# Turning the first x chunks on TensorE instead of in the DMA, in a fused linear-attention and FFN kernel

## The chip, the core and the metric

The kernel runs on one core of a Trainium2 chip. The metric is the device time of one execution in microseconds. The core has TensorE (PE: matmuls; PEld is its weight load, which overlaps the matmuls), VectorE (DVE), ScalarE (ACT), GpSimd (POOL) and SyncE (SP), which here only issues DMAs. Every engine has its own instruction stream, and the streams are tied together by semaphores. A DMA is issued by one engine's queue (SP's or ScalarE's here), moved by 16 DMA engines that all queues share, and tells of its landing by a semaphore.

## What is computed

The input x has 2048 tokens of 640 features in bf16. The output mixes two branches with a gate for each token: linear attention with a learned softmax feature map over 32 heads of 20 features, and a SwiGLU feed-forward net of width 1728.

```python
qkv = x @ wqkv                       # 32 heads, 20 features each
pq, pk = q @ w_phi, k @ w_phi        # per head
phi = concat(softmax(p), softmax(-p))
kv, z = phi_k^T @ v, sum(phi_k)
a = (phi_q @ kv / (phi_q @ z + 1e-6)) @ wo
b = (silu(x @ w_gate) * (x @ w_up)) @ w_down
g = sigmoid(sum(x * gate_w))
return g * a + (1 - g) * b
```

## The kernel before

**Layout.** All matmuls contract over the partitions, so x is needed with its features on the partitions: xT holds five chunks of 128 features by 2048 tokens. x lies in memory with the tokens first. Six DMA transposes bring it (line 515), by blocks of 512 tokens; the first block comes in three pieces, chunks 0 and 1, chunks 2 and 3, chunk 4. The weights w_gate and w_up (wg, wu) are loaded in pieces by chunk and by column, `k` being a block of 128 columns.

**Order.** The order of every engine's instructions is fixed when the program is built. `_Plan` (lines 238 to 334) is a list scheduler: each task has an engine, an estimated cost, dependencies, a priority, and sometimes an `after` (the task that must precede it on its engine), a `hold` (not before this planned time) or a `land` (when a DMA is taken to have landed). The planner walks through its own time, and emits each task's instructions when its turn comes. What the chip then does is bound to the order, not to the planned times: `_Tracker` (line 38) puts a semaphore wait ahead of an instruction wherever it reads or overwrites what another engine or DMA produced. The constants `L_SLACK`, `E_SLACK` and `O_SLACK` (line 484) are added to planned landings of loads and of two kinds of transposes; lines 713 to 720 hold planned start times of the key tiles (`K_AT`, `K_EACH`), of the query tiles (`Q_AT`, `Q_EACH`), ranks (`PRE_Q`), and how the feed-forward's down projections are threaded among the rest (`D_AFTER`).

**The head.** The loads of lines 540 to 564 are all issued by SP, one after another. The first are wg[0:2] for four blocks k (line 540), x chunks 0 and 1 transposed (541), wu[0:2] (542), wg[2:5] for k 0 and 1 (543), x chunks 2 to 4 transposed (544), wg[2:5] for k 2 and 3 (545), wu[2:5] (546), then the next weight pieces and the second block of x (547, 548). Meanwhile PE runs ten warm matmuls on a row of ones (lines 610 to 622), which compute nothing that is used. `ffn_head` (line 684) then computes gate and up projections of the first 512 tokens for four blocks k, in all eight PSUM banks, chunk by chunk in the order in which the pieces arrive: 8 matmuls for wg[0:2], 8 for wu[0:2], 4 and 2 for wg[2:4] and wg[4:5] with k 0 and 1, 6 for wg[2:5] with k 2 and 3, 12 for wu[2:5]. ScalarE (tanh), VectorE and GpSimd finish each block (`ffn_tail`, line 636).

**The rest.** Interleaved by the planner follow the rest of the feed-forward, value and key tiles, then the query tiles. In each query tile the features are normalised, transposed by a DMA (`eT`), multiplied with the key-value matrix, divided, transposed again (`oT`) and multiplied with wo. Scratch tensors that are needed only early (wqT, wbd, wph) share the slab in which the output tiles (xsb) are later collected (lines 403 to 409).

Of the kernel before, what the change touches and what calls it, by code (L numbers as in the profile page):

```python
# [6 lines left out]
P = 128  # L7
S_TOK = 2048
D = 640
H = 32  # L10
DH = 20
F_FFN = 1728
NT = S_TOK // P
# [12 lines left out]
PC = 6 * DH  # L26
NPC_W = 6
PHI_NH = (6, 6, 6, 6, 6, 2)
ACTF = mybir.ActivationFunctionType
ALU = mybir.AluOpType  # L30
AX = mybir.AxisListType
DT = mybir.dt
BF16 = DT.bfloat16
# [204 lines left out]
class _Plan:  # L238
# [11 lines left out]
    def add(self, eng, cost, fn, deps=(), prio=5.0, lat=None, acq=(), rel=(), name=""):  # L250
        t = _Task(eng, cost, fn, deps, prio, self.LAT[eng] if lat is None else lat,
                  tuple(acq), tuple(rel), len(self.tasks), name)
        self.tasks.append(t)
        return t
# [86 lines left out]
def _build(  # L341
# [13 lines left out]
    pe, act, dve, pool, sp = nc.tensor, nc.scalar, nc.vector, nc.gpsimd, nc.sync  # L355
# [13 lines left out]
    def sbat(name, shape, dtype, at):  # L369
        t = nc.alloc_sbuf_tensor_at(name, list(shape), dtype, offset=at)  # L370
        tr.reg_tensor(t, "sbuf", at, rowelems(shape), mybir.dt.size(dtype))
        return t

    xT = sb("xT", [P, 5, S_TOK], BF16)
# [29 lines left out]
    base = nc.lookup_mloc(slab).addr  # L404
# [2 lines left out]
    wqT = sbat("wqT", [P, 2 * NPC_W, D], BF16, base)  # L407
    wbd = sbat("wbd", [P, NPC_W, 6, DH], BF16, base + 2 * NPC_W * D * 2)
    wph = sbat("wph", [PC, NPC_W, DH], BF16, base + 2 * NPC_W * D * 2 + NPC_W * 6 * DH * 2)

    ps = nc.alloc_psum_tensor("ps", [P, 8 * 512], F32)
    tr.addr[ps.name] = ("psum", 0, 8 * 512, 4)

    x2 = A_x[0]
# [3 lines left out]
    add = plan.add  # L418
# [4 lines left out]
    def one(b, c0, c1, r0=0, r1=P):  # L423
        return ps[r0:r1, b * 512 + c0:b * 512 + c1]
# [4 lines left out]
    def mms(groups):  # L429

        reads = [g[1] for g in groups] + [g[2] for g in groups]
        writes = []
        seen = set()
        for g in groups:
            k = (g[0].offset, str(g[0].ap))
            if k not in seen:
                seen.add(k)
                writes.append(g[0])

        def fn():  # L440
            last = None
            for o, l, r, st, sp_ in groups:
                last = pe.matmul(o, lhsT=l, rhs=r, start=st, stop=sp_, skip_group_check=True)  # L443
            return last
        run("pe", fn, reads=reads, writes=writes)
# [5 lines left out]
    def actop(o, i, func, scale=1.0):  # L451
        reads = [i] + ([scale] if isinstance(scale, bass.AP) else [])
        run("act", lambda: act.activation(o, i, func, scale=scale), reads=reads, writes=[o])  # L453

    def dveop(fn, reads, writes):
        run("dve", fn, reads=reads, writes=writes)

    def poolop(fn, reads, writes):
        run("pool", fn, reads=reads, writes=writes)

    def memset(t_ap, val, eng):
        eobj = {"pool": pool, "dve": dve}[eng]
        run(eng, lambda: eobj.memset(t_ap, val), reads=[], writes=[t_ap])
# [17 lines left out]
    v1ones = places(v1all)[:, :, :, DH]  # L481
    v1pad = v1all.rearrange("p (g x) -> p g x", x=WIN)[:, :, WIN - 1]

    L_SLACK, E_SLACK, O_SLACK = 1.0, 1.8, 1.6
    chain = {}

    def load(eng, dst, src, land, prio, transpose=False, name="load", cost=0.06):

        t = add(eng, cost, lambda: dma(eng, dst, src, transpose=transpose), prio=prio, lat=2.0, name=name)
        t.land = land  # L490
        t.slack = L_SLACK if land > 13 else 0.0
        t.after = chain.get(eng)
        chain[eng] = t
        return t

    def rows(a):
        return a.rearrange("(c p) j -> p c j", p=P)
# [4 lines left out]
    wgl = [None] * (NPC + 1)  # L502
    wul = [None] * (NPC + 1)

    def load_gu(j, eng, land, prio):
        c0, c1 = PIECES[j]
        wgl[j] = load(eng, wg[:, :, c0:c1], gsrc[:, :, c0:c1], land[0], prio)
        wul[j] = load(eng, wu[:, :, c0:c1], usrc[:, :, c0:c1], land[1], prio + 0.1)

    def load_x(bt, prio, *cuts):  # L510

        tok = slice(512 * bt, 512 * bt + 512)
        out_ = []
        for i, (c0, c1, land) in enumerate(cuts):
            out_ += [load("sp", xT[:, c0:c1, tok], x2[tok, c0 * P:c1 * P], land, prio + 0.1 * i, True, "x%d" % bt)] * (c1 - c0)
        return out_

    def load_wT(which, land, prio):
        o = NPC_W * which
        col = [which * D + PC * c for c in range(NPC_W)]  # L520
        return [load("sp", wqT[:, o + c, :], A_wqkv[:, col[c]:col[c] + P], land - 1.0 * (NPC_W - 1 - c), prio + 0.01 * c, True, "wT") for c in range(NPC_W)]
# [8 lines left out]
    xs = [None] * NBT  # L530
    HD = 4
    hw = {}

    def load_head(key, c0, c1, k0, k1, land, prio):
        w, src = (wg, gsrc) if key == "g" else (wu, usrc)
        t = load("sp", w[:, c0:c1, k0 * P:k1 * P], src[:, c0:c1, k0 * P:k1 * P], land, prio)
        for k in range(k0, k1):
            hw[key, c0, k] = t
        return t
    load_head("g", 0, 2, 0, HD, 3.9, -43)  # L540
    xa = load_x(0, -42, (0, 2, 5.25))
    load_head("u", 0, 2, 0, HD, 6.9, -41)
    load_head("g", 2, 5, 0, 2, 7.4, -40.5)
    xs[0] = xa + load_x(0, -40, (2, 4, 8.8), (4, 5, 9.3))
    wgl[0] = load_head("g", 2, 5, 2, HD, 10.0, -39.5)
    wul[0] = load_head("u", 2, 5, 0, HD, 11.3, -39)
    load_gu(1, "sp", (12.5, 13.7), -37)
    xs[1] = load_x(1, -36.5, (0, 5, 16.4))
    phi_rows = A_w_phi.rearrange("h e f -> (h e) f")
    ph_l = [load("sp", wph[:, 0:5, :], phi_rows[0:5 * PC, :].rearrange("(c p) j -> p c j", p=PC), 16.5, -36.2),  # L550
            load("sp", wph[0:2 * DH, 5, :], phi_rows[5 * PC:D, :], 16.6, -36.1)]
    wkT_l = load_wT(1, 24.4, -36)
    wv_l = load("sp", wvg[:, :, 0:D], rows(A_wqkv[:, 2 * D:3 * D]), 26.8, -35)
    load_gu(2, "sp", (28.0, 29.2), -34)
    load_gu(3, "sp", (30.6, 32.0), -33)
# [9 lines left out]
    xl = [x_[4] for x_ in xs]  # L565

    zero = add("dve", 0.3, lambda: memset(us[:, 0, 0:2], 0.0, "dve"), prio=-20, name="zero")
    table = add("act", 1.3, lambda: actop(us[:, 1, 0:1], us[:, 0, 0:1], ACTF.Tanh), deps=[zero], prio=-20, name="table")  # L570
# [39 lines left out]
    def warm(banks, before):  # L610
        ctx = {}

        def fn():
            for b in banks:
                last = pe.matmul(one(b, 0, 512), lhsT=ones_row[:, 0:P], rhs=ones_row[:, 0:512], start=True, stop=True, skip_group_check=True)
            return last
        b0, b1 = min(banks), max(banks) + 1
        t = add("pe", 0.427 * len(banks), lambda: run("pe", fn, reads=[], writes=[ps[:, b0 * 512:b1 * 512]]), prio=-10,
                acq=[("bank", ctx, i) for i in range(b0, b1)], rel=[("bank", ctx, i) for i in range(b0, b1)], name="warm")
        t.after = before  # L620
        return t
    warm_t = warm((4, 5, 6, 7, 4, 5), warm((0, 1, 2, 3), None))


    gate_t = {}
# [58 lines left out]
    def ffn_head():  # L684
        tsl = slice(0, 512)
        cs = [{} for _ in range(HD)]
        before = warm_t
        last = {}

        def group(key, c0, c1, parts):  # L690
            nonlocal before
            w = wg if key == "g" else wu

            def fn(ks, cc):
                mms([(one(cs[k][key], 0, 512), w[:, c, P * k:P * k + P], xT[:, c, tsl], c == 0, c == 4) for c in cc for k in ks])
            for ks in parts:
                t = add("pe", _mm(*[512] * (len(ks) * (c1 - c0))), lambda ks=ks: fn(ks, range(c0, c1)),
                        deps=[xs[0][c1 - 1], hw[key, min(c0, 2), ks[-1]]], prio=-5,
                        acq=[("bank", cs[k], key) for k in ks] if c0 == 0 else (), name="head")
                t.after = before  # L700
                before = t
                for k in ks:
                    last[key, k] = t
        group("g", 0, 2, [(0, 1, 2, 3)])
        group("u", 0, 2, [(0, 1, 2, 3)])
        group("g", 2, 4, [(0, 1)])
        group("g", 4, 5, [(0, 1)])
        group("g", 2, 5, [(2, 3)])
        group("u", 2, 5, [(0,), (1,), (2,), (3,)])
        for k in range(HD):  # L710
            ffn_tail(0, k, cs[k], (last["g", k], last["u", k]), 0)

    B_FIRST = 8
    K_AT, K_EACH, Q_AT, Q_EACH = 29.00, 6.115, 119.64, 8.094
    PRE_Q = 10.05
    PRE_EACH = 2.0
    PRE_AT = 23.6
    D_AFTER = 3
    FIN_DVE = 12
    K_PAIRS = 9  # L720
    store_t = {}
# [297 lines left out]
    pre_k = premult(1, wkT_l, 2.0, at=PRE_AT)  # L1019
    pre_q = premult(0, wqT_l, PRE_Q, 0.02)  # L1020
    wq_done[0] = pre_q[-1]
# [9 lines left out]
    for bt in range(1, NBT):  # L1031
        ks = list(range(K_PAIRS if bt == 1 else 0, NK))
        ds = [("d", u, bt - 1) for u in range(4)]
        for i, k in enumerate(ks):
            seq.append(("f", k, bt))
            if i >= D_AFTER and ds:
                seq.append(ds.pop(0))
# [67 lines left out]
```

## Time and profile before

| What | Value |
|---|---|
| Time, median of 3 runs | 287.14 us (287.12 to 287.69) |
| Profiled execution, its own time | 287.02 us |
| Profiled execution, span from first to last instruction | 285.3 us |
| TensorE's granted clock | 1.000 |
| PE 128x512 matmul of the head, x528 | 379 ns each by the record, one started every 216 |
| Line 909, POOL, normalising the features, x32 | 77.6 us in all |
| Line 899, DVE, summing the features, x32 | 48.5 us in all |
| DMA, 24.23 MB | mean 85 GB/s over the span |

The profile is of one execution. An engine's busy share says how much of the span it worked. A timeline line gives start, length, engine, line of the program, operation, out<-in and how many instructions are merged. A matmul's record lasts longer than the time until the next can start, since matmuls are pipelined, so starts are to be compared, not lengths. In the tables by stretch, each line is a stretch in us, its length, then busy time and number of instructions of PE, PEld, DVE, ACT and POOL, the granted clock, the DMA engines' mean share and the GB/s. SPq and ACTq are the issuing queues of SyncE and ScalarE. PE's 40 head matmuls run from 4.88 to 13.80 us, and its last five matmuls from 282.51 to 282.95; a last VectorE operation and a store follow.

### The profile page before, as it was taken

The page shows a single profiled execution, that of the slowest core. Times are in us where ns is not written, and L with a number is a line of the kernel's source. Part 1 is how long each engine was busy: PE and PEld are TensorE (multiplying, and loading weights), DVE is VectorE, ACT ScalarE, POOL GpSimd, SP SyncE. Part 2 cuts the span into 40 slices and gives each one's busy share as a digit, 9 for nine tenths or more (in the row PEclk, how much of TensorE's full clock was granted, in tenths as well). Part 3 has the DMA queues.
Part 4 walks back from the last instruction along what each step waited for, and adds up shares of the span by engine and source line. Part 5 has one row for each costly group of instructions (what it writes and reads, how often), then busy time and mean ns, then how long its engine had stood idle before and what let it go on. Part 6 is the DMA issues. An engine that isn't in the chain of part 4 may idle for free.

```text
span 285.3 us, 5120 instructions
## 1 busy us (share of the span) xinstructions
PE 279.9 (98%) x2013; PEld 150.6 (53%) x2050; DVE 224.0 (79%) x318; ACT 145.5 (51%) x222; POOL 171.1 (60%) x168
## 2 busy tenths in 40 slices
PE   8999999999999999999999999999999999999996
PEld 3444555555545455655465555555545555445654
DVE  1324398998999997997999999899989898961312
ACT  2555567685566484334634454745655444662210
POOL 5199406839657666745675577697786656575100
DMA  7979997860000000000302447473444254033211
GB/s 171 262 124 241 202 211 150 255 201 0 2 0 2 0 2 0 2 0 0 53 2 52 97 102 117 75 141 77 99 97 77 60 112 88 11 76 74 71 46 46
DMA packets 67457, 24.23 MB, mean 85 GB/s; under 512 B 55593, under 2 KB 67433, under 8 KB 67433
## 3 DMA queue, kind: packets, MB, share of 16 engines
q1 hardware_dynamic: 66777, 23.91, 40.0%
q8 instruction: 16, 0.26, 0.4%
q10 hardware_dynamic: 656, 0.00, 0.1%
q14 instruction: 8, 0.07, 0.1%
HBM read 8.30 MB, written 2.62 MB: 38 GB/s over the span
## 4 chain that ended last, share of the span: by engine, by line
PE 95%; SPq 2%; DMA 1%; issue 1%; DVE 0%
PE ps L443 95%; SPq L471 2%; DMA wg<-in_B_w_gate_dram 1%; DVE xsb L745 0%
## 5 line engine op out<-in xcount | busy, mean ns | idle before, releaser
L909 POOL TENSOR_TENSOR phi<-phi,rc 128x1320 bf16<-128x1320 bf16 x32 | 77.6, 2425 | 32.7 <-DVE rc L903 32.7
L661 POOL TENSOR_TENSOR hT<-hT,us 128x512 bf16<-128x512 bf16 (+1 forms) x56 | 64.0, 1152 | 45.4 <-DVE hT L655 31.1
L443 PE MATMUL ps<-xT,wg 128*128 128x512 bf16 x271 | 67.3, 379 | 0.8
L443 PE MATMUL ps<-xT,wu 128*128 128x512 bf16 x257 | 63.6, 379 | 0.0
L443 PE MATMUL ps<-wd,hT 128*128 128x512 bf16 (+1 forms) x442 | 62.2, 298 | 0.3
L453 ACT ACTIVATE phi<-phi 128x1320 bf16<-128x1320 bf16 x32 | 41.7, 1303 | 24.9 <-DVE phi L888 24.9
L453 ACT ACTIVATE hT<-ps 128x512 bf16<-128x512 f32 (+1 forms) x56 | 33.2, 597 | 41.1 <-PE ps L443 40.8
L899 DVE TENSOR_REDUCE sm<-phi 128x66 f32<-128x1320 bf16 x32 | 48.5, 1518 | 5.7 <-ACT phi L453 5.4
L655 DVE SCALAR_TENSOR_TENSOR hT<-hT,ps 128x512 bf16<-128x512 bf16 (+1 forms) x56 | 37.5, 675 | 18.8 <-ACT hT L453 18.8
L443 PEld LDWEIGHTS ps<-wd,hT 128*128 128x128 bf16 x448 | 35.1, 98 | 27.6
L443 PE MATMUL ps<-wqk,xT 128*128 128x128 bf16 (+1 forms) x311 | 47.4, 297 | 0.5
L453 ACT ACTIVATE us<-ps 128x512 bf16<-128x512 f32 (+1 forms) x56 | 33.2, 598 | 17.6 <-PE ps L443 16.3
L443 PEld LDWEIGHTS ps<-xT,wu 128*128 128x128 bf16 x260 | 25.3, 98 | 30.8 <-DMA wu<-in_B_w_up_dram 0.3
L443 PEld LDWEIGHTS ps<-xT,wg 128*128 128x128 bf16 x280 | 25.5, 98 | 26.2 <-DMA wg<-in_B_w_gate_dram 0.6
L443 PEld LDWEIGHTS ps<-wqk,xT 128*128 128x128 bf16 x320 | 26.1, 98 | 21.0
L876 DVE TENSOR_REDUCE mx<-ps 128x33 f32<-128x660 f32 x32 | 26.6, 832 | 6.8 <-PE ps L443 6.8
L888 DVE TENSOR_TENSOR phi<-mn,ps 128x660 bf16<-128x660 f32 x32 | 26.3, 822 | 0.3
L884 DVE TENSOR_TENSOR phi<-ps,mx 128x660 bf16<-128x660 f32 x32 | 26.4, 825 | 0.0
L880 DVE TENSOR_REDUCE mn<-ps 128x33 f32<-128x660 f32 x32 | 26.2, 817 | 0.0
L453 ACT ACTIVATE xsb<-ps,gs 128x640 bf16<-128x640 f32 x16 | 12.7, 793 | 25.3 <-PE ps L443 25.3
L759 POOL TENSOR_TENSOR xsb<-xsb,xb 128x640 bf16<-128x640 bf16 x12 | 16.7, 1396 | 11.3 <-ACT xb L453 11.3
L443 PE MATMUL ps<-wo,oT 128*128 128x128 bf16 (+1 forms) x153 | 23.0, 295 | 0.4
(45 smaller groups left out, 187.1 us busy)
## 6 DMA issues: line engine op xcount, KB each, us to landing
out_dram<-xsb SPq DMA_DIRECT2D x15, 160.0 KB, 1.9
wd<-in_B_w_down_dram SPq DMA_DIRECT2D x1, 2080.0 KB, 10.5
wvg<-in_A_wqkv_dram SPq DMA_DIRECT2D x1, 800.0 KB, 5.9
wg<-in_B_w_gate_dram SPq DMA_DIRECT2D x2, 400.0 KB, 6.4
wu<-in_B_w_up_dram SPq DMA_DIRECT2D x2, 400.0 KB, 6.7
wo<-in_A_wo_dram SPq DMA_DIRECT2D x1, 800.0 KB, 10.9
wg<-in_B_w_gate_dram SPq DMA_DIRECT2D x2, 320.0 KB, 5.5
wu<-in_B_w_up_dram SPq DMA_DIRECT2D x2, 320.0 KB, 6.1
```

Source lines behind the costliest of these rows:

```text
L443: last = pe.matmul(o, lhsT=l, rhs=r, start=st, stop=sp_, skip_group_check=True)
L453: run("act", lambda: act.activation(o, i, func, scale=scale), reads=reads, writes=[o])
L471: fn = (lambda: eobj.dma_start(dst, src, transpose=True)) if transpose else (lambda: eobj.dma_start(dst, src))
L655: dveop(lambda: dve.scalar_tensor_tensor(out=hap, in0=hap, scalar=1.0, in1=g_, op0=ALU.add, op1=ALU.mult), [hap, g_], [hap])
L661: poolop(lambda: pool.tensor_tensor(hap, hap, u_, ALU.mult), [hap, u_], [hap])
L759: poolop(lambda: pool.tensor_tensor(x_, x_, b_, ALU.add), [x_, b_], [x_])
L876: dveop(lambda: dve.tensor_reduce(a, b, AX.X, ALU.max), [b], [a])
L880: dveop(lambda: dve.tensor_reduce(a, b, AX.X, ALU.min), [b], [a])
L884: dveop(lambda: dve.tensor_tensor(o_, a, b, ALU.subtract), [a, mx[:, ctx["st"], :]], [o_])
L888: dveop(lambda: dve.tensor_tensor(o_, a, b, ALU.subtract), [b, mn[:, ctx["st"], :]], [o_])
L899: dveop(lambda: dve.tensor_reduce(a, b, AX.X, ALU.add), [b], [a])
L909: poolop(lambda: pool.tensor_tensor(a, a, b, ALU.mult), [a, r], [a])
```

## The change

The first two chunks of x's first 512 tokens are no longer transposed by a DMA. Two plain DMAs on SP bring them with tokens on the partitions (xp, 4 tiles of 128 by 128 for each chunk, in rows of 256 bytes). PE turns each tile by a matmul against an identity matrix into PSUM; VectorE copies the first half of the tokens into xT, ScalarE the second. GpSimd builds the identity. xp and the identity lie in the slab. w_gate's first piece is split in two, one for each chunk, and ScalarE's queue issues both. The first gate group is split likewise. Of the ten warm matmuls six are left. The planned landings of the head's loads and several planner constants have new values.

```diff
-    L_SLACK, E_SLACK, O_SLACK = 1.0, 1.8, 1.6
+    L_SLACK, E_SLACK, O_SLACK = 1.0, 1.6, 1.4
...
-    load_head("g", 0, 2, 0, HD, 3.9, -43)
-    xa = load_x(0, -42, (0, 2, 5.25))
-    load_head("u", 0, 2, 0, HD, 6.9, -41)
-    load_head("g", 2, 5, 0, 2, 7.4, -40.5)
-    xs[0] = xa + load_x(0, -40, (2, 4, 8.8), (4, 5, 9.3))
-    wgl[0] = load_head("g", 2, 5, 2, HD, 10.0, -39.5)
-    wul[0] = load_head("u", 2, 5, 0, HD, 11.3, -39)
...
+    def load_xp(c, land, prio):
+        return load("sp", xp[:, c, :, :], x2[0:512, c * P:(c + 1) * P].rearrange("(t p) j -> p t j", p=P), land, prio)
+    load_head("g", 0, 1, 0, HD, 3.4, -43, "act")
+    load_head("g", 1, 2, 0, HD, 4.2, -42.9, "act")
+    xp_l = [load_xp(0, 3.35, -43), load_xp(1, 3.8, -42)]
+    load_head("u", 0, 2, 0, HD, 5.2, -41)
+    load_head("g", 2, 5, 0, 2, 5.8, -40.5)
+    xs[0] = [None, None] + load_x(0, -40, (2, 4, 7.3), (4, 5, 7.9))
+    wgl[0] = load_head("g", 2, 5, 2, HD, 8.9, -39.5)
+    wul[0] = load_head("u", 2, 5, 0, HD, 10.1, -39)
...
+    def build_ident():
+        memset(ident[:, :], 1.0, "pool")
+        for m, b in ((1, 0), (-1, 0)):
+            poolop(lambda m=m: pool.affine_select(
+                out=ident[:, :], in_=ident[:, :], pattern=[[-m, P]], compare_op=ALU.is_ge, fill=0.0,
+                base=0, channel_multiplier=m), [ident[:, :]], [ident[:, :]])
+    ident_t = add("pool", 0.8, build_ident, prio=-30, name="ident")
...
-    warm_t = warm((4, 5, 6, 7, 4, 5), warm((0, 1, 2, 3), None))
+    warm_t = warm((4, 5, 6, 7), warm((0, 1), None))
+
+    def turn(c, before):
+        ctx = {}
+
+        def fn():
+            mms([(one(ctx[i // 2], P * (i % 2), P * (i % 2) + P), xp[:, c, i, :], ident[:, :], True, True) for i in range(4)])
+        t = add("pe", 0.43, fn, deps=[xp_l[c], ident_t], prio=-10, acq=[("bank", ctx, 0), ("bank", ctx, 1)], name="turn")
+        t.after = before
...
+        ev.append(add("dve", 0.36, copy_d, deps=[t], prio=-30, rel=[("bank", ctx, 0)], name="turned"))
+        ev.append(add("act", 0.36, copy_a, deps=[t], prio=-30, rel=[("bank", ctx, 1)], name="turned"))
+        return t, ev
+    turn_t, xe0 = turn(0, warm_t)
+    turn_t, xe1 = turn(1, turn_t)
+    xe = [xe0, xe1]
...
-        group("g", 0, 2, [(0, 1, 2, 3)])
+        group("g", 0, 1, [(0, 1, 2, 3)])
+        group("g", 1, 2, [(0, 1, 2, 3)])
...
-    K_AT, K_EACH, Q_AT, Q_EACH = 29.00, 6.115, 119.64, 8.094
-    PRE_Q = 10.05
+    K_AT, K_EACH, Q_AT, Q_EACH = 29.00, 6.110, 120.29, 8.074
+    PRE_Q = 10.12
...
-    D_AFTER = 3
+    D_AFTER = 4
```

## The prediction, made before the changed kernel ran

> **What bounds the kernel now.** I read the page first: its busy shares, then the chain that ended last.
>
> ```profile
> span 285.3 us, 5120 instructions
> PE 279.9 (98%) x2013; PEld 150.6 (53%) x2050; DVE 224.0 (79%) x318; ACT 145.5 (51%) x222; POOL 171.1 (60%) x168
> PE 95%; SPq 2%; DMA 1%; issue 1%; DVE 0%
> ```
>
> TensorE is busy 98% of the span and makes 95% of the chain. Only the first few microseconds belong to something else (SP's issues and one DMA). Next, the busy time by stretches of 20 us:
>
> ```profile
> 64.00:84.00 20.00, 19.84 (x155) 10.82 (x157) 19.05 (x25) 12.33 (x23) 14.38 (x12) 1.00 0.00 1
> 104.00:124.00 20.00, 19.85 (x164) 11.20 (x167) 18.11 (x25) 9.35 (x14) 11.59 (x11) 1.00 0.01 2
> 224.00:244.00 20.00, 19.84 (x161) 11.23 (x162) 17.15 (x26) 10.22 (x13) 10.76 (x9) 1.00 0.46 97
> ```
>
> The first figure after the length is PE. It is 19.8 of 20 everywhere, and the 0.16 left over is three pauses of 0.05, which the chain calls issue. So from the head's end on nothing waits, and nothing can be won there; something can be lost. What can be won lies ahead of 13.8 us. The timeline of PE:
>
> ```profile
> 3.36 0.99 PE L615 MATMUL ps<-const-bfloat16-1.0 128*128 128x512 bf16 x2
> ...
> 3.79 1.00 PE L615 MATMUL ps<-const-bfloat16-1.0 128*128 128x512 bf16 x3
> 4.88 1.89 PE L443 MATMUL ps<-xT,wg 128*128 128x512 bf16 x8
> 6.61 1.89 PE L443 MATMUL ps<-xT,wu 128*128 128x512 bf16 x8
> 8.33 3.04 PE L443 MATMUL ps<-xT,wg 128*128 128x512 bf16 x12
> 11.21 2.54 PE L443 MATMUL ps<-xT,wu 128*128 128x512 bf16 x11
> 13.80 1.24 PE L443 MATMUL ps<-xT,wg 128*128 128x512 bf16 x5
> ```
>
> L615 are the ten warm matmuls on ones, L443 is work. Eight matmuls take 6.61 - 4.88 = 1.73 us, 0.216 each. Warm ones follow each other at 0.427 (3.36 to 3.79) until about 4.2 us, so the array runs at half its rate that long. The head's 40 matmuls need 40 x 0.216 = 8.64 us, but 4.88 to 13.80 is 8.92: 0.28 us of waiting. The waits name it:
>
> ```profile
> PEld ps L443 <- DMA wg<-in_B_w_gate_dram: 0.6, 1, 0.6
> ...
> PEld ps L443 <- DMA wu<-in_B_w_up_dram: 0.3, 1, 0.3
> ```
>
> The first is the piece wg[2:5, k 2-3], whose wait ends at 9.90 (the weight loader's 0.6 is partly under a running matmul). Last, what the DMA engines moved, by microsecond (the last two figures are DMA share and GB/s):
>
> ```profile
> 2.00:3.00 1.00, 1.00 (x4) 0.36 (x3) 0.45 (x3) 0.30 (x2) 0.86 (x4) 1.00 0.79 199
> 3.00:4.00 1.00, 1.00 (x4) 0.38 (x3) 0.63 (x2) 0.00 (x0) 0.86 (x4) 1.00 1.20 290
> 4.00:5.00 1.00, 0.91 (x4) 0.23 (x3) 0.00 (x0) 0.00 (x0) 0.61 (x2) 1.00 0.80 138
> 5.00:6.00 1.00, 1.00 (x6) 0.43 (x5) 0.00 (x0) 0.00 (x0) 0.00 (x0) 1.00 0.98 281
> ```
>
> At full stream the loads make 280 to 290 GB/s, with transposes (3 to 4) and without (5 to 6). Behind the transposed x chunks the rate falls to 138 (126 in 4.0 to 4.9).
>
> **The sum as a rule.** The head's end is the later of two: start T plus 8.64 if no weight is late, or the old 13.80 less s, where s is by how much the stream brings wg[2:5, k 2-3] earlier (18 matmuls stand behind that piece either way). Gain = the smaller of 13.80 - 8.64 - T = 5.16 - T, and s.
>
> **T, the start of useful work.** The six warm matmuls left end at about 0.84 + 0.38 + 5 x 0.427 = 3.36. In before the first weight piece, 256 KB, was issued at 0.81 and landed 2.9 us later, at 3.7; while it moved, the array was waiting for x, issued at 1.33, landed 3.4 us later at 4.73, and the first matmul came at 4.88. Now xp chunk 0 (SP) and wg chunk 0 (ScalarE's queue) go first, 256 KB together, so 3.7 bounds their landing above; packets first moved at 1.9, and 128 KB at 288 GB/s is 0.46 us, so 2.4 bounds it below. I take 3.3, near the upper one, since both queues use the same engines. Then turn 0 starts when the warm ones end, 3.36; four 128-column matmuls at half rate (the wide-form row spacing, 0.427/4) take 0.43; their end reaches a copy about 0.3 later. ScalarE's copy of 256 columns lies between its 512-column row (597 ns) and its 4-column row (199): 0.40. VectorE's, from PSUM at 320 and 384 columns (483 and 558 ns), extends to 0.41. With 0.05 to hand on, T = 3.36 + 0.43 + 0.3 + 0.41 + 0.05 = 4.55. Turn 1 stands ahead of the first gate group on PE, and it waits for xp chunk 1: the other 256 KB, 0.91 us behind at 288 GB/s, so 4.2 (bounds 3.3 and 4.6), plus at most 0.43: 4.4 to 5.0. I take T = 4.55; its bounds are 4.45 and 5.0, so 5.16 - T is 0.61, between 0.16 and 0.71. Chunk 1's copies (0.4) hide behind the four gate matmuls of chunk 0 (0.86). Without that cover they cost up to 0.7.
>
> **s, the stream.** SP issued its first transposed x in 1.32 us and the first weight piece in 0.46; both leave its front, and two plain issues of about 0.5 each come instead, so u's and all later pieces are issued 0.85 earlier (u at 1.9 instead of 2.71). The bytes are the same, 1.5 MB up to the piece in question. The slack behind the first transposes goes: 0.9 us at 126 GB/s instead of 288 is 0.5 us. So s is 0.5 to 0.85 if 256-byte rows move like the rest, and I take 0.65. No row shows a plain 256-byte load. Transposed packets of that size went at 288 GB/s (3.3 to 4.0); 512-byte rows at 287 (5.4 to 6.2). If each costs as much as a 512-byte one, 256 KB take 1.83 us and not 0.91, and s is -0.4 to -0.05. The transposed row is nearest in size, so I keep 0.65.
>
> The Trainium skill, "DMA: Bandwidth & Descriptors", section Specifications, speaks against this choice: it asks for at least 512 bytes per transfer at line rate, with a read-modify-write below. By it s would be near its lower end and the time 287.1 to 287.5, by the transposed row 286.5; no run here shows which.
>
> **What costs nothing.** The identity is three GpSimd operations, some 0.9 us by its rows (a 126-column memset 0.21, selects 0.35), done by 1.8; it pushes pads and masks, and GpSimd then sat idle 8.45 us to 13.14. Uncovered it would cost PE as much as it ends after 3.36. ScalarE's two issues are 0.45 each, ahead of its table load (1.28) and its copies at 4.1; if the load came first and held them, weights land about 1.3 later, 4.6, and T is 4.6 to 4.7, a loss of 0.1. SP and the ScalarE queue are passed by no other early DMA; the gate_w load comes at 9.84. The copies find VectorE idle from 3.65. Behind the waiting turns on PE stands the whole head; behind their copies on ScalarE and VectorE nothing until 9.8. The turned chunks cost PE 8 x 0.056 to 0.107 = 0.45 to 0.86 us, which lies in the time before T, where four warm matmuls (1.7 us) went out.
>
> **The new plan constants** (E_SLACK, O_SLACK, Q_AT, PRE_Q, D_AFTER) reorder work behind the head. PE used the transposed eT tiles 0.6 us or more after they landed, mostly 2 to 4, and oT 1.5 or more, so 0.2 us less in the planner's slack is covered. If the cover is gone, each late tile is a stall on PE. I take 0 here, bounds 0 and +1.5.
>
> **Sum.** min(0.61, 0.65) = 0.6. The profiled execution took 287.02 (285.3 span, 1.7 around it), the runs' median is 287.14: 286.4 to 286.55, I say 286.5.
>
> **Rivals.** Changes within 0.2% (0.57 us) can't be told from none.
> 1. *Weights as late as before.* The array starts at 4.6 but waits for wg[2:5, k 2-3], since small rows are slow or turn 1 gets xp chunk 1 late. For it: no row for such a load, and today's wait is on that piece. Against: 0.85 us of SP's issue is gone. Gain -0.4 to 0.4, by the bounds of s: 286.7 to 287.5.
> 2. *The array stays at half rate* (slower side). Place: between 3.4 and 4.6 PE now has pauses, where it ran without one up to 4.8. Full rate came 3.3 us after the first warm matmul (4.2 against 0.84). If the pauses start that count anew from T, 3.3/0.427 = 7.8 matmuls run where 15.5 would: 7.7 x 0.216 = 1.66 lost, less the 0.6 won, +1.05: 288.1. It decides once xp chunk 0 lands more than some tenths after 3.36. Against: the warm ones still fill 3.4 of the first 4.2 us.
> 3. *The new order stalls PE later.* VectorE is busy 18 to 19 of 20 us in the middle, so a worse order has little room. One stall a tile of 0.1 us over 16 query tiles is 1.6, less 0.6: 288.0. Against: cover of 0.6 to 4 us.
>
> The Trainium skill, "TensorE: Matmul & The Clock Gate", Part 1, has rival 2 as a rule: half clock until a window of some 3.4 us was busy, the window running freely. The trace agrees with half rate (0.427 and 0.216 us) and with 3.3 us once; no run here shows what pauses do.
>
> **Chances.** Forecast 0.50, rival 1 0.28, rival 2 0.11, rival 3 0.11. The likeliest gives 286.5 (own range 286.3 to 286.8). The range goes from 286.2 to 287.9: under it little, as T cannot be below 4.45; above it about half of rivals 2 and 3. Faster by over 0.2% means under 286.57: 0.48 (most of the forecast, a little of the rest). Slower means over 287.71: 0.20, most of rivals 2 and 3. The rest, 0.32, is the same.
>
> **What would show it.** PE's timeline: six L615 matmuls to 3.4, eight narrow ones, the first L443 with wg at 4.55, the first after the head (13.80 now) at 13.2. The waits: no PEld wait on wg at 9.9. Spacing 0.216 from T on, else rival 2. The 20 us stretches: 19.8 again, else rival 3. The issues: wg[2:5, k 2-3] landing at 9.2 rather than 9.86; if it still lands at 9.8, rival 1. The prediction is wrong if T is over 4.9 or any stretch behind 14 us is under 19.7.

## The result and the profile after

The changed kernel took 289.12 us (median of 22 runs, 287.14 to 290.24) where the kernel before took 287.26 (22 runs, 286.9 to 287.78). The ratio is 1.0044, with a 95% interval of 1.0029 to 1.006: slower, where 286.5 was forecast. The single runs say more than the median. Ten lie between 287.14 and 287.48, twelve between 289.12 and 290.24, and none between. So there are two questions: why the lower ten won nothing, and what costs the other twelve some 2.3 us.

The profiled execution belongs to the lower ten (287.48, span 285.8). Its page, busy shares and chain:

```profile
span 285.8 us, 5140 instructions
PE 282.1 (99%) x2054; PEld 151.0 (53%) x2054; DVE 225.5 (79%) x320; ACT 145.9 (51%) x224; POOL 172.5 (60%) x171
...
PE 98%; DMA 1%; SPq 0%; DVE 0%; issue 0%
```

The share called issue is gone, and with it the 0.05 us pauses of the kernel before. They were no pauses. Here 2054 matmul records stand for 2054 weight loads, in before 2013 for 2050: each "pause" was a lost record, as the gap between starts there is longer by 0.216, the spacing of one matmul.

PE's timeline over the head:

```profile
2.51 1.06 PE L632 MATMUL ps<-const-bfloat16-1.0 128*128 128x512 bf16 x2
3.83 0.61 PE L447 MATMUL ps<-ident,xp 128*128 128x128 bf16 x4 [0.27 <-DMA xp<-in_A_x_dram]
4.66 0.60 PE L447 MATMUL ps<-ident,xp 128*128 128x128 bf16 x4 [0.22 <-DMA xp<-in_A_x_dram]
5.05 2.07 PE L447 MATMUL ps<-xT,wg 128*128 128x512 bf16 x8
6.96 1.89 PE L447 MATMUL ps<-xT,wu 128*128 128x512 bf16 x8
8.69 2.75 PE L447 MATMUL ps<-xT,wg 128*128 128x512 bf16 x12
11.28 2.75 PE L447 MATMUL ps<-xT,wu 128*128 128x512 bf16 x12
13.87 0.59 PE L447 MATMUL ps<-xT,wg 128*128 128x512 bf16 x2
```

The warm matmuls end at 3.36 as worked out. Both turns wait for xp (the brackets), the first gate matmul comes at 5.05 instead of 4.88, and the head ends at 13.87 instead of 13.80. The turns' four matmuls are 0.107 apart, half rate. Full rate comes at about 5.4, read off the first gate matmul, which is followed after 0.397, and from then on every 0.216.

The DMA issues of four pieces, one line each from the issues view of that piece's moment (KB, then us from issue to landing; SP's timeline has them start at 0.80, 1.32, 1.86 and 6.26):

```profile
xp<-in_A_x_dram SPq DMA_DIRECT2D x1, 128.0 KB, 3.0
...
xp<-in_A_x_dram SPq DMA_DIRECT2D x1, 128.0 KB, 3.3
...
wu<-in_B_w_up_dram SPq DMA_DIRECT2D x1, 256.0 KB, 4.6
...
wg<-in_B_w_gate_dram SPq DMA_DIRECT2D x1, 192.0 KB, 3.7
```

xp lands at 3.8 and 4.6. wu, issued 0.85 earlier than before, lands at 6.4 as before (6.3), and wg[2:5, k 2-3] at 9.9 (9.86 before). wu's earlier issue bought nothing. wg[2:5, k 2-3] itself was issued only 0.16 earlier (6.26 instead of 6.42), since the two transposes ahead of it took SP 3.3 us to issue instead of 2.5.

### The profile page after: what moved, and what is told of

It is laid out like the page before. It is cut to its first block, busy times and chain, and to the rows that moved or that the text cites. A ratio compares the mean times of both kernels' runs of the same rounds, so it can differ in the third digit from the quotient of the medians.

```text
span 285.8 us, 5140 instructions
## 1 busy us (share of the span) xinstructions
PE 282.1 (99%) x2054; PEld 151.0 (53%) x2054; DVE 225.5 (79%) x320; ACT 145.9 (51%) x224; POOL 172.5 (60%) x171
## 4 chain that ended last, share of the span: by engine, by line
PE 98%; DMA 1%; SPq 0%; DVE 0%; issue 0%
PE ps L447 98%; DMA xp<-in_A_x_dram 1%; SPq L475 0%; DVE xsb L789 0%
## 5 line engine op out<-in xcount | busy, mean ns | idle before, releaser
L447 PE MATMUL ps<-xT,wg 128*128 128x512 bf16 x280 | 69.3, 380 | 0.0
L447 PE MATMUL ps<-xT,wu 128*128 128x512 bf16 x260 | 64.3, 379 | 0.0
L447 PE MATMUL ps<-wd,hT 128*128 128x512 bf16 (+1 forms) x448 | 63.0, 299 | 0.0
L447 PE MATMUL ps<-wqk,xT 128*128 128x512 bf16 (+1 forms) x320 | 48.5, 299 | 0.0
L447 PE MATMUL ps<-wo,oT 128*128 128x512 bf16 (+1 forms) x160 | 24.4, 299 | 0.0
## 6 DMA issues: line engine op xcount, KB each, us to landing
wo<-in_A_wo_dram SPq DMA_DIRECT2D x1, 800.0 KB, 10.2
```

## The experiments

Edits of the head that would have moved the planner's order (dummy matmuls, a load in another form) were given the same planned cost as what they replace, so the instruction order of all else is the changed kernel's or the old one's, whichever is named. The row of before is that beside the first four; beside the others it took 287.30 and 287.32. "Full rate" is the time from which 512-column matmuls are 0.216 and no longer 0.427 us apart, in the one profile of each.

| Run | Runs, median (range), us | Ratio (95%) | First gate matmul | Full rate |
|---|---|---|---|---|
| before | 34, 287.28 (286.91 to 287.81) | | 4.88 | 4.2 |
| after_again | 12, 289.31 (287.38 to 289.91) | 1.0045 (1.0024 to 1.0067) | 5.17 | 9.7 |
| after_10warm | 12, 288.38 (287.51 to 288.78) | 1.0032 (1.0022 to 1.0043) | 5.31 | 3.6 |
| after_fill | 12, 287.68 (287.31 to 288.22) | 1.0015 (1.0007 to 1.0024) | 5.19 | 5.9 |
| before_6warm | 11, 288.80 (286.99 to 289.26) | 1.0045 (1.0032 to 1.0058) | 5.02 | 8.0 |
| before_newconst | 11, 287.17 (286.91 to 287.68) | 0.9997 (0.9989 to 1.0006) | 5.1 | 6.4 |
| after_oldconst | 7, 289.51 (287.93 to 290.39) | 1.0061 (1.0036 to 1.0086) | 5.23 | 8.2 |
| after_512row | 6, 289.56 (287.88 to 290.1) | 1.0069 (1.0046 to 1.0092) | 5.54 | 9.0 |
| before_act | 11, 287.56 (287.1 to 287.72) | 1.0006 (0.9997 to 1.0014) | 5.1 | 6.4 |
| after_512_fill | 11, 288.10 (287.76 to 288.28) | 1.0021 (1.0013 to 1.0030) | 5.89 | by 5.7 |
| after_512_fill_sp | 12, 287.88 (287.76 to 288.51) | 1.0023 (1.0014 to 1.0032) | 5.54 | 3.6 |

**The changed kernel again (after_again)**, with no edit.

> The changed kernel once more, for a second profile. Its 22 runs lay in two groups, 287.1 to 287.5 and 289.1 to 290.2 us. Clock theory: the array reaches full rate only after a stretch without long pauses, and the changed head has pauses of 0.5 and 0.4 us between 3.4 and 4.7; in about half of the executions full rate comes a stretch later. Expected: two groups again, and a profile of the upper group would show matmuls 0.427 us apart until 8 to 11 us and everything behind 14 us as in the lower group. Order theory: the new plan's order falls into stalls later; a profile of the upper group would show 0.216 from 5.5 on and stretches behind 14 us with some 2 us less PE time.

Two groups again: five runs from 287.38 to 287.58, seven from 289.22 to 289.91. The profile fell into the upper one. PE's timeline:

```profile
3.88 0.60 PE L447 MATMUL ps<-ident,xp 128*128 128x128 bf16 x4 [0.32 <-DMA xp<-in_A_x_dram]
4.78 0.61 PE L447 MATMUL ps<-ident,xp 128*128 128x128 bf16 x4 [0.29 <-DMA xp<-in_A_x_dram]
5.17 3.62 PE L447 MATMUL ps<-xT,wg 128*128 128x512 bf16 x8
8.59 2.43 PE L447 MATMUL ps<-xT,wu 128*128 128x512 bf16 x8
...
13.44 2.75 PE L447 MATMUL ps<-xT,wu 128*128 128x512 bf16 x12
```

The first eight gate matmuls take 8.59 - 5.17 = 3.42 us where the other profile has 1.91. The last head group begins at 13.44, not 11.28: 2.16 us late, and the span is 2.1 longer (287.9 against 285.8). All of the upper group's loss is in the head. The table by microsecond counts it: in this profile

```profile
6.00:7.00 1.00, 1.00 (x4) 0.42 (x3) 0.00 (x0) 0.00 (x0) 0.00 (x0) 1.00 0.93 153
7.00:8.00 1.00, 1.00 (x4) 0.34 (x3) 0.00 (x0) 0.00 (x0) 0.00 (x0) 1.00 1.17 236
```

and in the first profile of the changed kernel

```profile
6.00:7.00 1.00, 1.00 (x7) 0.43 (x5) 0.00 (x0) 0.00 (x0) 0.00 (x0) 1.00 0.94 141
7.00:8.00 1.00, 1.00 (x6) 0.46 (x5) 0.00 (x0) 0.00 (x0) 0.00 (x0) 1.00 1.26 243
```

PE is "1.00 busy" in both, but starts four matmuls in a microsecond instead of six or seven. The granted clock (the 1.00 ahead of the DMA share) is the same in both: this column does not show the half rate. The order theory falls.

**Ten warm matmuls (after_10warm).** The loop over the second call's banks runs twice; nothing else moves.

```diff
-            for b in banks:
+            for b in banks * (2 if len(banks) == 4 else 1):
```

> The changed kernel with ten warm matmuls instead of six, the order of all else unchanged. Clock theory: PE runs without a pause to 4.4 us as before, the upper group is gone; the turns start at about 4.4 instead of 3.83, the head ends at the later of its stream bound 13.87 and about 14.2, so 287.2 to 287.9 in one group. Order theory: still two groups, about 2.3 us apart.

Nothing above 288.78: the runs that stood at 289 to 290 are gone. The price is a later start, and more of it when the ten run at half rate to their end (0.84 + 10 x 0.427 = 5.1) than in the profiled case (full rate at 3.6). Five of the twelve runs lie within the 287.2 to 287.9 that was expected, seven lie above it, from 288.28 to 288.78, for that reason as far as the one profile can tell.

**Fill the pauses (after_fill).**

```diff
+            run("pe", lambda: pe.matmul(one(ctx[0], 0, 512), lhsT=ones_row[:, 0:P], rhs=ones_row[:, 0:512], start=True, stop=True, skip_group_check=True), writes=[one(ctx[0], 0, 512)])
             mms([(one(ctx[i // 2], P * (i % 2), P * (i % 2) + P), xp[:, c, i, :], ident[:, :], True, True) for i in range(4)])
```

> The changed kernel with one more dummy matmul on ones ahead of each of the two turns (into the bank that the turn then overwrites), so that PE has no pause longer than 0.1 us up to the first gate matmul; the order of all else unchanged. Clock theory: one group at 287.1 to 287.5, full rate from 4.2 us in most executions. Order theory: two groups as in the changed kernel.

```profile
3.36 0.63 PE L645 MATMUL ps<-const-bfloat16-1.0 128*128 128x512 bf16 x1
3.90 0.61 PE L447 MATMUL ps<-ident,xp 128*128 128x128 bf16 x4
4.30 0.63 PE L645 MATMUL ps<-const-bfloat16-1.0 128*128 128x512 bf16 x1
4.79 0.61 PE L447 MATMUL ps<-ident,xp 128*128 128x128 bf16 x4
5.19 2.26 PE L447 MATMUL ps<-xT,wg 128*128 128x512 bf16 x8
```

Two matmuls that compute nothing take the median from 289.3 to 287.68, with no upper group: 287.31 to 288.22. Full rate came at 5.9, though, not at 4.2 as expected, and only four of the twelve runs lie within the expected 287.1 to 287.5. A spread of 0.9 us is left that runs without pauses share.

**The kernel before with six warm matmuls (before_6warm).**

```diff
-            for b in banks:
+            for b in banks[2:]:
```

> The kernel before with six warm matmuls instead of ten, the order of all else unchanged, so that PE pauses from 3.4 to 4.88 us and nothing else is changed. Clock theory: a part of the executions goes up by 1.5 to 3 us, two groups. Order theory: no difference to the kernel before, 287.26, since the warm matmuls compute nothing and the order is the old one.

```profile
2.50 1.06 PE L615 MATMUL ps<-const-bfloat16-1.0 128*128 128x512 bf16 x2
5.02 3.34 PE L443 MATMUL ps<-xT,wg 128*128 128x512 bf16 x8 [1.46 <-DMA xT<-in_A_x_dram]
8.20 1.89 PE L443 MATMUL ps<-xT,wu 128*128 128x512 bf16 x8
```

One run stays at 286.99, ten go to 288.23 to 289.26. Nothing was touched but four matmuls without a use. With the fill, this pins the loss from both sides: pauses put in bring it, pauses taken out remove it.

**The planner constants alone (before_newconst) and undone (after_oldconst).** The four changed lines of constants from the diff, put into the kernel before, and taken back in the changed one.

> The kernel before with the planner constants of the changed one (E_SLACK, O_SLACK, K_EACH, Q_AT, Q_EACH, PRE_Q, D_AFTER), head untouched. Behind the head the changed kernel shows five PE pauses of 0.05 to 0.12 us, 0.3 to 0.35 in all, at the same places in four profiles. If the constants cause them, this kernel has pauses of that size and 287.4 to 287.8, in one group; if they come of the head's new planned times, 287.26. Clock theory in both: no upper group, PE runs without a pause to 4.4.

> The changed kernel with the old planner constants. Clock theory: two groups as in the changed kernel, some 2.3 us apart, since the head is the same. If the new constants cause the later pauses, both groups lie 0.3 lower; if the old constants do not fit the new head, both lie higher and the profile shows where.

On the old head the new constants cost nothing (0.9997, interval 0.9989 to 1.0006). On the new head the old ones are worse: the lowest group is 287.93 to 288.17 against 287.14 to 287.58, and its profile has two waits that the changed kernel lacks, 0.28 us at 55.3 and 0.4 at 173.5. The changed kernel's own later waits, five of 0.05 to 0.12 us (at 90.8, 143, 156.5, 158.6 and 256.8, found again, shifted by what the head took, in the six profiles with this order that recorded every matmul), appear only with the new head: the old head under the new constants has none. Under the old constants the new head has others. So they come with the new head as it is planned (its tasks and its planned landings); which part of it was not tried.

**xp in 512-byte rows (after_512row).** One load for both chunks; xp's shape and the turn's index into it follow.

```diff
-        return load("sp", xp[:, c, :, :], x2[0:512, c * P:(c + 1) * P].rearrange("(t p) j -> p t j", p=P), land, prio)
+        return load("sp", xp[:, :, :], x2[0:512, 0:2 * P].rearrange("(t p) j -> p t j", p=P), land, prio)
...
-    xp_l = [load_xp(0, 3.35, -43), load_xp(1, 3.8, -42)]
+    xp_l = [load_xp(3.35, -43)] * 2
```

> The changed kernel with the two xp loads as one, in 512-byte rows (512 of them instead of 1024 of 256 bytes), order of all else unchanged. If the small rows hold the stream back, wg[2:5, k 2-3] lands by 9.4 instead of 9.92 and the lower group falls by up to 0.4. If they do not, it lands at 9.8 to 9.9 and the lower group stays at 287.1 to 287.5. Clock theory: turn 0 waits for the whole 256 KB, a longer pause from 3.4, so at least as many executions in the upper group.

wg[2:5, k 2-3], issued at 5.25, has this line:

```profile
wg<-in_B_w_gate_dram SPq DMA_DIRECT2D x1, 192.0 KB, 3.6
```

It lands at 8.9, not 9.9: the stream is 1.0 us earlier. That does not show the rows to be the cause, because the single load also saves SP one issue, so that all later ones start earlier. The first wu piece, in the changed kernel and then here:

```profile
1.86 0.50 SPq L475 DMA_DIRECT2D wu<-in_B_w_up_dram  x1
...
1.32 0.49 SPq L475 DMA_DIRECT2D wu<-in_B_w_up_dram  x1
```

wg[2:5, k 2-3] follows at 5.25 instead of 6.26. What the rows cost by themselves is small: 256-byte rows of xp moved at 286 GB/s (after_again, 2.8 to 3.0 us, 215 of 218 packets under 512 bytes), 512-byte rows at 342 (this kernel, 9.6 to 10.2), which is an estimated 0.15 us on 256 KB. The last figure of these rows (GB/s) shows where the stream gained, first in this kernel,

```profile
3.00:4.00 1.00, 0.56 (x2) 0.00 (x0) 0.62 (x2) 0.23 (x2) 0.86 (x4) 1.00 1.12 362
4.00:5.00 1.00, 0.67 (x7) 0.68 (x8) 0.03 (x1) 0.03 (x1) 0.86 (x4) 1.00 1.04 335
```

then in the changed kernel:

```profile
3.00:4.00 1.00, 0.73 (x4) 0.17 (x3) 0.65 (x2) 0.24 (x2) 0.86 (x4) 1.00 1.18 295
4.00:5.00 1.00, 0.78 (x8) 0.52 (x6) 0.42 (x1) 0.38 (x1) 0.86 (x4) 1.00 0.80 192
```

It doesn't help the time, since both turns now wait for all 256 KB (4.3), the pause from 3.4 is 1 us, and five of six runs are in the upper group.

**ScalarE's issue alone (before_act).** The kernel before, wg[0:2] issued by ScalarE (`load_head` is given the argument for it).

```diff
-    load_head("g", 0, 2, 0, HD, 3.9, -43)
+    load_head("g", 0, 2, 0, HD, 3.9, -43, "act")
```

> The kernel before with one part of the change alone: wg[0:2] in one piece issued by ScalarE's queue, so SP starts with the transposed x chunks, 0.52 us earlier; ten warm matmuls, order of all else unchanged. If SP's issue time holds the stream back, u and wg[2:5, k 2-3] land 0.3 to 0.5 earlier, the first gate matmul comes at 4.4 to 4.5 and the time is 286.8 to 287.0. If the 16 DMA engines hold it back, T is earlier but wg[2:5, k 2-3] lands at 9.8 as before and the time stays 287.2 to 287.3.

Neither branch as a whole. x, issued at 0.80 rather than 1.33, still landed at 4.74 (4.75 before); wu, issued 0.52 earlier, landed at 6.9 (6.3 before); and wg[2:5, k 2-3] landed at 10.2, where the unchanged head has it at 9.86 to 10.36 in three profiles (before, before_6warm, before_newconst). T was not earlier either: the ten warm matmuls ran at half rate to their end, and the first gate matmul came right behind them, at 5.06. Half a microsecond of SP's issue time did not, by itself, hold the stream back.

**Both mended (after_512_fill), and one piece moved (after_512_fill_sp).** The 512-byte rows, two dummy matmuls ahead of the turns and one behind them. The helper `fill` and the edit of the rows are left out here.

```diff
+            if c == 0:
+                fill(one(ctx[0], 0, 512), 2)
             mms([(one(ctx[i // 2], P * (i % 2), P * (i % 2) + P), xp[:, i, P * c:P * c + P], ident[:, :], True, True) for i in range(4)])
...
+                if key == "g" and c0 == 0:
+                    fill(one(cs[ks[0]][key], 0, 512), 1)
```

> The changed kernel with xp in one load of 512-byte rows and PE kept busy: two dummy matmuls ahead of the turns, one behind them (in the bank that the first gate group then overwrites). Order of all else unchanged. Stream and clock theory together: wg[2:5, k 2-3] lands at 8.9 as in the kernel with 512-byte rows, no pause over 0.3 us, so no upper group; the first gate matmul at 5.3 to 5.6 sets the head's end, 13.9 to 14.3, and the later pauses of 0.3 stay: 287.3 to 288.2 in one group. If it still has an upper group, pauses are not what decides.

> As the one before, but the second half of wg's first piece is issued by SP behind xp instead of by ScalarE, so that xp shares the DMA engines with 128 KB less. Expected if that sharing delays xp: xp lands at about 3.9 instead of 4.28, the first gate matmul at 5.0 to 5.2, the time 0.3 lower than the one before, 287.0 to 287.9. If ramp or latency sets xp's landing, no difference.

PE's timeline of the first, the dummy matmul behind the turns and the first gate group:

```profile
5.66 0.39 PE L644 MATMUL ps<-const-bfloat16-1.0 128*128 128x512 bf16 x1 [0.22 <-DVE xT L664]
5.89 1.89 PE L447 MATMUL ps<-xT,wg 128*128 128x512 bf16 x8
```

No upper group in either, the stream early in the first (9.0), and yet 1.0021 and 1.0023: xp landed at 4.5, the dummy matmul came at 5.66 and the first gate matmul at 5.89, later than the 5.3 to 5.6 that was expected, and 5.89 + 8.64 = 14.53 is the head's end (14.52 in the profile), 0.7 behind the old one. The second one's expectation failed. xp landed at 4.35, hardly earlier, the first gate matmul came at 5.54, and wg[2:5, k 2-3] landed at 9.7, though its xp rows are 512 bytes as well. That is within the 9.6 to 9.9 of the five profiles with 256-byte rows. SP has as many issues here as in the changed kernel, and wu goes out at 1.86 again. So the rows alone are not shown to bring the stream forward. What else makes the first wu piece land at 5.4 to 5.6 in two of these kernels and at 6.2 to 6.9 in the others stays open: an earlier issue alone did not do it in the changed kernel or in before_act.

## Why the prediction was wrong, step by step

- **T.** The step "I take 3.3" for xp's first landing failed, and with it turn 1: xp landed at 3.8, just over its bound of 3.7, and at 4.6, on the upper bound of chunk 1. Turn 1, right ahead of the first gate matmul, then set T (4.66 to 5.05; chunk 0's copies were done at 4.90). T is 5.05 instead of 4.55, past the upper bound of 5.0.
- **s.** The steps "the slack behind the first transposes goes" and "u's and all later pieces are issued 0.85 earlier" failed. u was issued 0.85 earlier and landed no earlier; the piece that counts was issued 0.16 earlier. The slack moved: 192 GB/s instead of 138 from 4 to 5 us, but 141 instead of 267 from 6 to 7. s is -0.06, and 0.05 to 0.26 in the four other profiles with the same loads, all against one landing of the old head (9.86), whose own loads landed as late as 10.36 (before_newconst); by the middle landing of three profiles of the old head and of five of the new one (9.89 and 9.68) it is about 0.2, not 0.65.
- **The rows in s.** The choice of the transposed row as the nearest was not what failed: xp's 256-byte rows moved at 286 GB/s, transposed ones at 288, and the price of a 512-byte row for each was not paid. The Trainium skill's line rate of at least 512 bytes ("DMA: Bandwidth & Descriptors", Specifications) has the right direction, 286 against 342 GB/s here, but that is worth an estimated 0.15 us on 256 KB. (The prediction's 287 for 512-byte rows is from a stretch with 84 smaller packets among 452.)
- **min(5.16 - T, s)** came out right as a number: 5.16 - 5.05 = 0.11 and -0.06 give -0.06, and the head ended 0.07 later. By its path that is partly luck. PE paused nowhere between 5.05 and 13.87: 5.05 + 8.64 = 13.69, and the first gate matmul, still at half rate for most of its time (0.397 instead of 0.216), adds 0.18, a term that the rule lacks. The weight piece, loaded at 9.96 for a matmul at 9.98, would have given the same end.
- **The half-rate rival** was named with the right place and price (1.66 worked out, 1.63 if 3.3 is divided by 0.427 and 0.216; 2.16 in the profile) and given 0.11. It took 12 of 22 runs. Its weighing failed: "full rate came 3.3 us after the first warm matmul" was one execution. In the profiles without a long pause it came at 3.6 to 6.4, in those with pauses at 5.4 to 9.7. "It decides once xp chunk 0 lands more than some tenths after 3.36" was right: it landed 0.4 after. The step that put cover on the removed warm matmuls, "in the time before T", counted their cost and not what they were there for.
- **The new order at 0**, bounds 0 and 1.5: the profile has 0.35 us of new waits. With the head's 0.07 that is most of the 0.5 by which its span is longer (285.8 against 285.3). These are two single executions, the slowest of the lower ten (287.48) and one of the faster ones of the kernel before (287.02). The middle of the lower ten, 287.27, is that of the kernel before, 287.26. The prediction's pauses of 0.05 in the kernel before were lost records, as shown above.
- **Right:** the end of the warm matmuls, the identity and the copies (0.38 and 0.42 us) hidden, ScalarE's issues at 0.81 and 1.26 ahead of its table load at 1.75, and all that could be won lying ahead of 13.8 us.

## What to carry to other kernels

Work that computes nothing may hold the array at its rate: before taking warm matmuls out, or putting a wait behind them, fill every pause until the real work, and look at the matmuls' spacing in more than one profile. With a race between two arrivals, win on both or win nothing: here the start and the weight stream each had to come earlier, and an earlier issue is not by itself an earlier landing. Read single runs before a median, since a cost that falls on half of the executions shows as two groups.

## What was not expected of the hardware

- The array's full rate came anywhere from 3.6 to 6.4 us in seven profiles with pauses of at most 0.35 us ahead of it, in kernels with the same start (0.84), so 2.7 to 5.6 us after it. That it varies fits the freely running window in the Trainium skill ("TensorE: Matmul & The Clock Gate", Part 1). The Trainium skill has the array busy for some 3.4 us first; the 2.7 us of two profiles (after_10warm, after_512_fill_sp) are less, and the measurement decides. The variation can also account for much of the spread of the kernel before: its order profiled with full rate at 4.2 took 287.02, the same head (before_newconst) with 6.4 took 287.52.
- With pauses of 0.4 to 1.7 us in the first 5 us full rate came at 5.4 once and at 8.0 to 9.7 in four more profiles. The longer the pauses, the more executions stood in the upper group: 23 of 41 with two pauses of 0.4 to 0.6 us (the changed kernel, after_again, after_oldconst), 5 of 6 with one of 1.0 (after_512row), 10 of 11 with one of 1.7 (before_6warm). Once full rate had come, two pauses of 0.5 us did not end it (after_512_fill_sp). How busy a window must be stays open.
- The profile's granted clock is 1.00 throughout, at half rate too.
- The first wu piece moved slowly for most of a microsecond in two kernels (126 GB/s from 4.0 to 4.9 in before, behind transposes; 192 from 4 to 5 in the changed kernel, with none ahead), but not in after_512row (335 from 4 to 5). The cause stays open.
